# Attention by halves of the heads: logits with stationary masks in four column groups, values accumulated in transposed form

## The chip, the cores and the metric

The kernel runs on one core of one Trainium2 chip. The metric is the device time of one execution in microseconds (us). PE is TensorE, the matmul engine (PEld its weight loads), DVE is VectorE, ACT is ScalarE, POOL is GpSimd, SP the queue that starts transfers. In a matmul one operand stands still in PE (stationary, brought in by a weight load) and the columns of the other are moved past it; an eviction is the copy of a result out of the accumulator memory, PSUM. Four column groups are four matmuls of 32 stationary columns each, written 128*32 in the traces, whose results go to four separate sets of 32 rows. The granted clock (PEclk) is the share of its full clock that PE was given. Kernels are compared only within the same rounds.

## The reference, cut to what matters

Four layers in a row over x of 2048 tokens and 512 features: state-space convolution (A), attention (B), A, B. Only the attention changes.

```python
def _B_ref(x, wqkv, wo):              # x is already layer-normalised
    H = 32; Dh = 16; W, dil = 8, 2
    q, k, v = split(x @ wqkv)         # [32 heads, 2048, 16] each
    idx = pos[:, None] - (arange(W) * dil)[None, :]     # 8 keys: 0, 2, ... 14 tokens back
    logits = einsum("bhsd,bhswd->bhsw", q, k[idx]) * Dh ** -0.5    # masked to -1e9 where idx < 0
    attn = softmax(logits)            # over 8 keys
    o = einsum("bhsw,bhswd->bhsd", attn, v[idx])
    return o.reshape(B, S, D) @ wo    # the residual is added outside
```

With 8 keys per token there is no large matrix of logits. VectorE multiplies q by a shifted k elementwise; PE sums the 16 features of each head with a mask matrix ("bones"); softmax runs over 8 values; VectorE multiplies V by the probabilities, and PE sums the 8 shifts by accumulating matmuls against the identity.

## The kernel before: the parts that matter

Token t lies at partition t // 16, index j = t % 16. "ft" counts blocks of 8 heads (128 features), "fp" the two halves of the heads.

```python
def proj_qk(fp):
    for which, dst in ((0, qT[fp]), (1, kT[fp])):          # q first, then k
        for f2 in range(2):
            for sh2 in range(2):                            # whole sequence inside
                ps = psA.tile([128, 1024], F32)
                # ... 2 x 4 matmuls of 512 columns ...
                nc.scalar.copy(dst[:, f2, sh2*1024:(sh2+1)*1024], ps[:])

def qk_products(fp):
    for jh in range(2):                                     # half of the tokens
        Lp = [psL.tile([128, W, 8, 8], F32) for _ in range(2)]
        for w in range(W):
            pr = work.tile([128, 2, 1024], BF, tag="prodqk", bufs=3)
            # ... VectorE: pr = qT * (kT shifted by 2*w), one or two instructions ...
            for f2 in range(2):
                for jj in range(8):                         # product stationary, 8 columns move
                    nc.tensor.matmul(Lp[f2][:, w, jj, :], pr[:, f2, jj*128:(jj+1)*128], bones[:], ...)
        for f2 in range(2):
            nc.scalar.copy(Lsb[:, :, j0:j0+8, ft*8:(ft+1)*8], Lp[f2][:])

proj_qk(0); proj_qk(1); qk_products(0); proj_v(); qk_products(1)
# sm_pre, sm_post: softmax by halves of the tokens, all 32 heads together

def pv_group(g):                                            # 4 of the 16 token indices, all heads
    for w in range(W):
        p2 = work.tile([128, 4, D], BF, tag="prodpv", bufs=3)
        # ... VectorE: p2 = V (or its shifted copy Vp) * probabilities ...
        for jj in range(4):                                 # identity stationary, 512 columns move
            nc.tensor.matmul(po[jj//2][:, jj%2, :], ident[:], p2[:, jj, :], start=(w==0), stop=(w==7))
    # ... ScalarE: o = po

def out_group(g):
    # ... PE: 16 transposes of o, ScalarE: oT = transposes ...
    # ... PE: 5 matmuls per token index (4 of wo, 1 adds X), ScalarE: X = result

sm_pre(0); sm_pre(1); sm_post(0); pv_group(0); pv_group(1); sm_post(1)
out_group(0); pv_group(2); out_group(1); pv_group(3); out_group(2); out_group(3)
```

Instructions are emitted in this program order, but the framework that builds the kernel settles each engine's own order from this order and from what is ready.

Of the kernel before, what the change touches and what calls it, by code (L numbers as in the profile page):

```python
# [20 lines left out]
H = 32  # L21
# [51 lines left out]
def make_consts(nc, const, C):  # L73
    fc = _fft_consts()
    bones_np = np.zeros((128, 8), dtype=np.float32)
    for f in range(128):
        bones_np[f, f // 16] = 1.0
    for name in ("F1", "F1T"):
        C[name + "_h"] = nc.inline_tensor(_bf(fc[name]), name="c_" + name)
    todo = [("ident", _bf(np.eye(128)), BF), ("C2", _bf(fc["C2"]), BF), ("IC", _bf(fc["IC"]), BF),  # L80
            ("bones", _bf(bones_np), BF), ("onesr", _bf(np.ones((1, 128))), BF)]
    for i, (name, arr, dt) in enumerate(todo):
        h = nc.inline_tensor(arr, name="c_" + name)
        t = const.tile(list(arr.shape), dt, name="sb_" + name)
        nc.sync.dma_start(t[:], h.ap())
        C[name] = t
# [16 lines left out]
def store_x(nc, X, out2d):  # L103
    ov = out2d.rearrange("(p j) d -> p j d", j=NJ)
    for g in range(NG):
        (nc.sync if g % 2 == 0 else nc.scalar).dma_start(ov[:, g * 4:(g + 1) * 4, :], X[:, g * 4:(g + 1) * 4, :])


def load_b_weights(nc, tc, const, wqkv, wo):
# [14 lines left out]
    Vp = const.tile([128, NJ, D], BF, name="Vp")  # L124
    nc.vector.memset(Vp[:, 0:2, :], 0.0)
    nc.gpsimd.memset(Vp[0:1, 2:NJ, :], 0.0)
# [453 lines left out]
def b_layer(nc, tc, C, X, Wt, Vp, ln_b):  # L580
    with ExitStack() as es:
        big = es.enter_context(tc.tile_pool(name="b_big", bufs=4))
        qk = es.enter_context(tc.tile_pool(name="b_qk", bufs=1))
        small = es.enter_context(tc.tile_pool(name="b_small", bufs=2))
        work = es.enter_context(tc.tile_pool(name="b_work", bufs=2))
        sm = es.enter_context(tc.tile_pool(name="b_sm", bufs=1))
        psA = es.enter_context(tc.tile_pool(name="b_psA", bufs=2, space=PSUM))
        psT = es.enter_context(tc.tile_pool(name="b_psT", bufs=2, space=PSUM))
        psL = es.enter_context(tc.tile_pool(name="b_psL", bufs=2, space=PSUM))
# [4 lines left out]
        for g in range(NG):  # L594
            for j in range(g * 4, g * 4 + 4):
                ln_b.norm(xn[:, j, :], X[:, j, :], j)
            for hf in range(2):
                pt = psT.tile([128, 2, 4, 128], BF, name="pt_x", tag="psT")
                for jj in range(2):
                    j = g * 4 + hf * 2 + jj  # L600
                    for ct in range(4):
                        nc.tensor.transpose(pt[:, jj, ct, :], xn[:, j, ct * 128:(ct + 1) * 128], ident[:])
                s0 = (g * 4 + hf * 2) * 128
                nc.scalar.copy(xnT[:, :, s0:s0 + 256].rearrange("c t (jj p) -> c jj t p", jj=2), pt[:])  # L604
# [3 lines left out]
        def proj_qk(fp):  # L608
            for which, dst in ((0, qT[fp]), (1, kT[fp])):
                for f2 in range(2):  # L610
                    ft = fp * 2 + f2
                    for sh2 in range(2):
                        ps = psA.tile([128, 1024], F32, name="ps_qk", tag="psA")
                        for sc in range(2):
                            s0 = (sh2 * 2 + sc) * 512
                            for ct in range(4):
                                nc.tensor.matmul(ps[:, sc * 512:(sc + 1) * 512],  # L617
                                                 wqk[:, ct, which * 512 + ft * 128: which * 512 + (ft + 1) * 128],
                                                 xnT[:, ct, s0:s0 + 512], start=(ct == 0), stop=(ct == 3))
                        nc.scalar.copy(dst[:, f2, sh2 * 1024:(sh2 + 1) * 1024], ps[:])  # L620

        V = big.tile([128, NJ, D], BF, name="V", tag="big")

        def proj_v():
            for jp in range(NJ // 2):
                ps = psA.tile([128, 2, D], F32, name="ps_v", tag="psA")
                for jj in range(2):
                    j = jp * 2 + jj
                    for ct in range(4):
                        nc.tensor.matmul(ps[:, jj, :], xnT[:, ct, j * 128:(j + 1) * 128], wv[:, ct, :],  # L630
                                         start=(ct == 0), stop=(ct == 3))
                nc.scalar.copy(V[:, jp * 2:(jp + 1) * 2, :], ps[:])
            nc.sync.dma_start(Vp[1:113, 2:NJ, :], V[0:112, 2:NJ, :])
            nc.sync.dma_start(Vp[113:128, 2:NJ, :], V[112:127, 2:NJ, :])

        Lsb = sm.tile([128, W, NJ, H], BF, name="Lsb")

        def qk_products(fp):
            for jh in range(2):
                j0 = jh * 8  # L640
                Lp = [psL.tile([128, W, 8, 8], F32, name="Lp", tag="psL") for _ in range(2)]
                for w in range(W):
                    sh = DIL * w
                    pr = work.tile([128, 2, 8 * 128], BF, name="prodqk", tag="prodqk", bufs=3)
# [13 lines left out]
                    for f2 in range(2):  # L658
                        for jj in range(8):
                            nc.tensor.matmul(Lp[f2][:, w, jj, :], pr[:, f2, jj * 128:(jj + 1) * 128], bones[:],  # L660
                                             start=True, stop=True)
                for f2 in range(2):
                    ft = fp * 2 + f2
                    nc.scalar.copy(Lsb[:, :, j0:j0 + 8, ft * 8:(ft + 1) * 8], Lp[f2][:])

        proj_qk(0)
        proj_qk(1)
        qk_products(0)
        proj_v()
        qk_products(1)  # L670

        for w in range(1, W):
            nc.vector.memset(Lsb[0:1, w, 0:DIL * w, :], -1e9)
        def sm_pre(jh):
            js = slice(jh * 8, (jh + 1) * 8)
            m1 = small.tile([128, 4, 8, H], BF, name="sm_m1", tag="sm_m1")
            nc.vector.tensor_tensor(m1[:], Lsb[:, 0:4, js, :], Lsb[:, 4:8, js, :], ALU.max)
            m2 = small.tile([128, 2, 8, H], BF, name="sm_m2", tag="sm_m2")
            nc.vector.tensor_tensor(m2[:], m1[:, 0:2], m1[:, 2:4], ALU.max)
            mx = small.tile([128, 8, H], BF, name="sm_mx", tag="sm_mx")  # L680
            nc.vector.tensor_tensor(mx[:], m2[:, 0], m2[:, 1], ALU.max)
            nc.vector.tensor_tensor(Lsb[:, :, js, :], Lsb[:, :, js, :],
                                    mx[:].unsqueeze(1).to_broadcast([128, W, 8, H]), ALU.subtract)
            nc.scalar.activation(Lsb[:, :, js, :], Lsb[:, :, js, :], ACT.Exp, scale=DH ** -0.5)

        def sm_post(jh):
            js = slice(jh * 8, (jh + 1) * 8)
            s1 = small.tile([128, 4, 8, H], BF, name="sm_s1", tag="sm_m1")
            nc.vector.tensor_tensor(s1[:], Lsb[:, 0:4, js, :], Lsb[:, 4:8, js, :], ALU.add)
            s2 = small.tile([128, 2, 8, H], BF, name="sm_s2", tag="sm_m2")  # L690
            nc.vector.tensor_tensor(s2[:], s1[:, 0:2], s1[:, 2:4], ALU.add)
            den = small.tile([128, 8, H], F32, name="sm_den", tag="sm_den")
            nc.vector.tensor_tensor(den[:], s2[:, 0], s2[:, 1], ALU.add)
            rdb = small.tile([128, 8, H], BF, name="sm_rdb", tag="sm_rdb")
            with nc.allow_low_precision(reason="softmax 1/sum kept in bf16 like the reference"):
                nc.vector.reciprocal(rdb[:], den[:])
            nc.vector.tensor_tensor(Lsb[:, :, js, :], Lsb[:, :, js, :],
                                    rdb[:].unsqueeze(1).to_broadcast([128, W, 8, H]), ALU.mult)

        prob = Lsb  # L700

        o = big.tile([128, NJ, D], BF, name="o", tag="big")
        oT = big.tile([128, 4, S], BF, name="oT", tag="big")

        def pv_group(g):
            j0 = g * 4
            po = [psA.tile([128, 2, D], F32, name="po", tag="psA") for _ in range(2)]
            for w in range(W):
                sh = DIL * w
                p2 = work.tile([128, 4, D], BF, name="prodpv", tag="prodpv", bufs=3)  # L710
                ja = max(j0, sh)
                if ja < j0 + 4:
                    n = j0 + 4 - ja
                    nc.vector.tensor_tensor(  # L714
                        p2[:, ja - j0: ja - j0 + n, :].rearrange("p j (t d h) -> p (j t) d h", t=4, d=DH),
                        V[:, ja - sh: ja - sh + n, :].rearrange("p j (t d h) -> p (j t) d h", t=4, d=DH),
                        prob[:, w, ja: ja + n, :].rearrange("p j (t h) -> p (j t) h", t=4).unsqueeze(2)
# [110 lines left out]
```

## Time and profile before

The time is 694.17 us (median of 3, 694.14 to 697.09).

| second attention layer, before | us |
|---|---|
| length, first normalisation to last residual write | 147.0 |
| PE busy | 114.6 |
| VectorE busy | 94.5 |
| ScalarE busy | 64.4 |

The first attention layer lasts 147.1 us. The next lines are the busy times by stretches of the second layer: the whole layer, projections, logits with most of the softmax, and values with output. Columns: stretch in us from the start of the span, its length, then busy us (and number of instructions) of PE, PEld, DVE, ACT and POOL, then the clock granted to PE, the share of the DMA engines, GB/s.

```profile
core 0: us, PE busy (x) PEld busy (x) DVE busy (x) ACT busy (x) POOL busy (x), PEclk, DMA share, GB/s
540.70:687.70 147.00, 114.57 (x1024) 62.41 (x1040) 94.46 (x121) 64.41 (x67) 0.00 (x0) 0.88 0.08 24
540.70:576.00 35.30, 33.92 (x223) 18.34 (x228) 9.17 (x22) 23.28 (x24) 0.00 (x0) 0.94 0.00 1
576.00:626.10 50.10, 28.05 (x541) 19.58 (x545) 45.26 (x61) 17.62 (x20) 0.00 (x0) 0.73 0.14 38
626.10:687.70 61.60, 52.60 (x266) 24.49 (x271) 40.03 (x40) 23.51 (x24) 0.00 (x0) 0.97 0.07 27
```

No engine is full. In the first stretch PE works and VectorE stands; in the second VectorE works and PE is half idle. The layer is a sequence of phases. The waits of VectorE in the same layer (in total us, times, longest) name the holes:

```profile
DVE prodqk L648 <- ACT kT_7272 L620: 14.9, 1, 14.9
DVE prodqk L648 <- PE Lp L660: 12.7, 2, 11.2
DVE prodpv L714 <- PE po L728: 8.0, 2, 4.8
```

The first is the wait for the first k projection, which comes after all of q. In the second, VectorE's three product buffers are full because the logits matmuls that free them are queued behind the projections of the other half of the heads. PE's timeline of the first layer shows that queue, up to 319.6 us, where VectorE's products had stopped at 308.8 and went on at 320.0:

```profile
295.90 23.69 PE L617 MATMUL ps_qk<-xnT,wqk 128*128 128x512 bf16 x107
```

### The profile page before, as it was taken

To read this page: it belongs to the slowest core of one execution; us is meant where nothing else is said; L and a number is where in the kernel's file an instruction comes from. 1 tells how busy PE (TensorE), PEld (TensorE's weight loads), DVE (VectorE), ACT (ScalarE), POOL (GpSimd) and SP (SyncE) were. 2 spreads that over 40 slices of the span, in tenths; PEclk is the share of its full clock that TensorE was granted. 3 is DMA by queue.
4 is the path that set the end of the run, shared out by engine and by line. 5 is a ranking of instruction groups with operands and counts; after the bars stand their busy time and mean duration, and the time that the engine had idled before them with its cause. 6 is when DMAs were issued, how large, how long until landed. Compare 5 with 4: busy or idle time off the path is not lost. (4 is left out here: it accounts for less than half of the span.)

```text
span 691.4 us, 13674 instructions
## 1 busy us (share of the span) xinstructions
PE 465.4 (67%) x5930; PEld 297.7 (43%) x5977; DVE 512.5 (74%) x984; ACT 331.3 (48%) x388; POOL 8.2 (1%) x21
## 2 busy tenths in 40 slices
PE   1103656866767875599834898787796699725996
PEld 0002444544645654445521444465664446512442
DVE  6999999989989932624998985864456526989870
ACT  5980525636637454565312435555442555331335
POOL 0000000000000003000000000000000000000000
PEclk9999959979979988899955999899999899857999
DMA  9000010210210214000210000500000000300001
GB/s 307 4 0 2 32 32 2 93 33 13 82 32 19 78 63 152 1 1 1 67 43 0 1 0 4 241 1 1 1 1 0 1 1 2 106 1 1 31 31 62
DMA packets 14541, 26.69 MB, mean 39 GB/s; under 512 B 4753, under 2 KB 10258, under 8 KB 13074
## 3 DMA queue, kind: packets, MB, share of 16 engines
q1 hardware_dynamic: 11792, 23.57, 9.8%
q10 hardware_dynamic: 2688, 2.23, 1.1%
q8 instruction: 47, 0.77, 0.5%
q14 instruction: 14, 0.11, 0.1%
HBM read 13.77 MB, written 8.39 MB: 32 GB/s over the span
## 5 line engine op out<-in xcount | busy, mean ns | idle before, releaser
L728 PE MATMUL po<-prodpv,sb_ident 128*128 128x512 bf16 x248 | 65.7, 396 | 36.2 <-DVE prodpv L714 31.3
L617 PE MATMUL ps_qk<-xnT,wqk 128*128 128x512 bf16 x248 | 56.6, 379 | 1.1 <-ACT xnT L604 0.7
L193 PE MATMUL psA<-U,sb_F_128 128*128 128x128 bf16 x256 | 24.1, 242 | 47.5 <-issue 38.5
L180 ACT CAST Z<-psA 128x1024 bf16<-128x1024 f32 (+1 forms) x52 | 46.4, 960 | 20.1 <-issue 17.3
L728 PEld LDWEIGHTS <-sb_ident 128*128 128x128 bf16 x256 | 25.7, 101 | 67.5 <-issue 45.2
L180 ACT CAST xc<-psA 128x1024 bf16<-128x1024 f32 x32 | 32.0, 1012 | 44.6 <-PE psA L222 37.4
L193 PEld LDWEIGHTS <-sb_F_128 128*128 128x128 bf16 x416 | 27.1, 104 | 57.9 <-issue 50.7
L208 PE MATMUL pt<-sb_ident,Z 128*128 128x128 bf16 x384 | 38.4, 268 | 19.5 <-ACT Z L180 19.5
L714 DVE TENSOR_TENSOR prodpv<-V,Lsb 128x2048 bf16<-128x2048 bf16 (+1 forms) x40 | 42.2, 1111 | 8.2 <-PE po L728 8.0
L180 ACT CAST VT<-psA 128x512 bf16<-128x512 f32 x48 | 26.6, 588 | 44.4 <-PE psA L250 44.4
L208 PEld LDWEIGHTS <-Z 128*128 128x128 bf16 x384 | 32.8, 123 | 30.4 <-ACT Z L180 21.9
L660 PE MATMUL Lp<-sb_bones,prodqk 128*128 128x8 bf16 x1024 | 35.3, 167 | 14.7 <-DVE prodqk L656 9.4
L660 PEld LDWEIGHTS <-prodqk 128*128 128x128 bf16 x1024 | 32.9, 99 | 24.3 <-DVE prodqk L656 10.8
L247 PE MATMUL psA<-sb_IC,pa 128*128 128x256 bf16 x128 | 36.2, 283 | 9.6 <-DVE pa L262 9.6
L159 DVE TENSOR_SCALAR U<-X,ln_rstd_a,ln_nb_a 128x128 bf16<-128x128 bf16 x128 | 33.5, 307 | 7.2 <-PE psA L193 7.2
L617 PEld LDWEIGHTS <-wqk 128*128 128x128 bf16 x256 | 24.7, 98 | 29.3 <-issue 1.6
L178 DVE COPY zt<-pt 128x1024 bf16<-128x1024 bf16 x32 | 21.8, 688 | 20.6 <-PE pt L208 20.5
L248 PE MATMUL psA<-sb_IC,pb 128*128 128x256 bf16 x128 | 36.2, 283 | 1.1 <-DVE pb L263 1.1
L745 PE MATMUL ps_o<-wo_t,oT 128*128 128x512 bf16 x124 | 32.3, 379 | 6.7 <-ACT o L731 4.3
L249 PE MATMUL psA<-sb_IC,pb 128*128 128x256 bf16 x128 | 36.0, 281 | 0.0
L250 PE MATMUL psA<-sb_IC,pa 128*128 128x256 bf16 x128 | 35.9, 281 | 0.0
L467 PE MATMUL psk<-Ytab,Xtab 128*32 128x64 bf16 x1024 | 23.6, 207 | 14.4 <-issue 7.1
(175 smaller groups left out, 1100.4 us busy)
## 6 DMA issues: line engine op xcount, KB each, us to landing
Kt<-kt_scratch SPq DMA_DIRECT2D x4, 1024.0 KB, 6.9
Vp<-V SPq DMA_DIRECT2D x2, 1568.0 KB, 8.9
kt_scratch<-Kt SPq DMA_DIRECT2D x3, 1024.0 KB, 3.8
X<-in_A_u_dram SPq DMA_DIRECT2D x4, 512.0 KB, 5.5
k_scratch<-KTq SPq DMA_DIRECT2D x8, 256.0 KB, 2.0
KT<-k_scratch SPq DMA_DIRECT2D x8, 256.0 KB, 2.7
sb_F_128<-c_F SPq DMA_DIRECT2D x1, 1024.0 KB, 5.9
sb_F1T<-c_F1T SPq DMA_DIRECT2D x1, 1024.0 KB, 7.1
```

The source lines that it names most:

```text
L159: self.nc.vector.tensor_scalar(dst, src, self.rstd[:, j:j + 1], self.nb[:, j:j + 1], ALU.mult, ALU.add)
L180: self.nc.scalar.copy(dst, src)
L193: nc.tensor.matmul(o, F1[:, j, r, :], rhs_j(j), start=True, stop=not dk)
L208: nc.tensor.transpose(pt[:, r, g, :], Z[:, r, i * 4 + g, :], ident[:])
L247: nc.tensor.matmul(o, pa[:, 0, sl], IC[:, 0, :], start=True, stop=False)
L248: nc.tensor.matmul(o, pb[:, 1, sl], IC[:, 1, :], start=False, stop=False)
L249: nc.tensor.matmul(o, pb[:, 0, sl], IC[:, 2, :], start=False, stop=False)
L250: nc.tensor.matmul(o, pa[:, 1, sl], IC[:, 2, :], start=False, stop=True)
L617: nc.tensor.matmul(ps[:, sc * 512:(sc + 1) * 512], wqk[:, ct, which * 512 + ft * 128: which * 512 + (ft + 1) * 128], xnT[:, ct, s0:s0 + 51 ...
L660: nc.tensor.matmul(Lp[f2][:, w, jj, :], pr[:, f2, jj * 128:(jj + 1) * 128], bones[:], start=True, stop=True)
L714: nc.vector.tensor_tensor(p2[:, ja - j0: ja - j0 + n, :].rearrange("p j (t d h) -> p (j t) d h", t=4, d=DH), V[:, ja - sh: ja - sh + n, :] ...
L728: nc.tensor.matmul(po[jj // 2][:, jj % 2, :], ident[:], p2[:, jj, :], start=(w == 0), stop=(w == W - 1))
```

## The change

Its intent: make logits cheaper on PE, get rid of the transposes of o, and let the two halves of the heads overlap, so that one engine's phase covers the other's. The core of the diff, with cuts marked:

```diff
-    bones_np = np.zeros((128, 8), dtype=np.float32)
+    bones_np = np.zeros((128, 4, 32), dtype=np.float32)
     for f in range(128):
-        bones_np[f, f // 16] = 1.0
+        for k in range(4):
+            bones_np[f, k, 8 * k + f // 16] = 1.0
 # ... small and work pools: 4 product buffers shared by logits and values; PSUM split anew ...
 # ... xnT: every second eviction goes to VectorE instead of ScalarE ...
-            for which, dst in ((0, qT[fp]), (1, kT[fp])):
-                for f2 in range(2):
-                    for sh2 in range(2):                 # 1024-column evictions
+            for sh2 in range(2):
+                for which, dst in ((1, kT[fp]), (0, qT[fp])):
+                    for f2 in range(2):                  # 512-column evictions
 # ... in qk_products:
-                    for f2 in range(2):
-                        for jj in range(8):
-                            nc.tensor.matmul(Lp[f2][:, w, jj, :], pr[:, f2, jj * 128:(jj + 1) * 128], bones[:],
-                                             start=True, stop=True)
+                    for hb in range(2):
+                        for f2 in range(2):
+                            r0 = (hb * 2 + f2) * 32
+                            nc.tensor.matmul(Lp[r0:r0 + 32, w // 4, :], bones[:, w % 4, :],
+                                             pr[:, f2, hb * 512:(hb + 1) * 512], start=(w % 4 == 0),
+                                             stop=(w % 4 == 3), skip_group_check=True)
+                LT = small.tile([128, 2, 4, 128], BF, name="LT", tag="LT", bufs=2)
+                nc.scalar.copy(LT[:]..., Lp[:]...)
+                # 8 PE transposes of LT into pt, then
+                nc.scalar.copy(L[fp][:, :, j0:j0 + 8]..., pt[:]...)
 # ... softmax(fp): by halves of the heads; the edge memsets go to GpSimd ...
 # ... pv(fp, jh): half of the heads and half of the tokens per block:
-                for jj in range(4):
-                    nc.tensor.matmul(po[jj // 2][:, jj % 2, :], ident[:], p2[:, jj, :],
-                                     start=(w == 0), stop=(w == W - 1))
+                for f2 in range(2):
+                    for jj in range(8):
+                        nc.tensor.matmul(po[f2][:, jj, :], p2[:, jj, f2 * 128:(f2 + 1) * 128], ident[:],
+                                         start=(w == 0 and jj % 4 == 0), stop=(w == W - 1), skip_group_check=True)
+            for f2 in range(2):
+                nc.scalar.copy(oT[:, fp * 2 + f2, j0 * 128:(j0 + 8) * 128], po[f2][:]...)
 # ... out(jh): no transposes; stores each 4 token indices as soon as they are done ...
         proj_qk(0)
+        qk_products(0)
         proj_qk(1)
-        qk_products(0)
+        softmax(0)
         proj_v()
         qk_products(1)
+        softmax(1)
+        pv(0, 0)
+        pv(0, 1)
+        pv(1, 0)
+        out(0)
+        pv(1, 1)
+        out(1)
```

So there are three parts: a new form of the logits on PE (the mask stationary, 512 product columns moving, four 32-row outputs in four column groups), a new form of the values (the product stationary, the result already transposed), and a new structure (halves of the heads throughout, and a new order).

## The prediction

> **What bounds the kernel now.** The change touches only the two attention layers. By the timeline each lasts 147 us from first normalisation to last residual write (284.9 to 432.0, 540.7 to 687.7); the rest stays. By stretches of time, in the second layer VectorE is busy 94.5 of 147 us, PE 114.6, ScalarE 64.4: nothing is full, the layer is a sequence of phases. In the first 35.3 us (projections) PE is busy 33.9, VectorE 9.2; in the next 50.1 us (logits, softmax) VectorE 45.3, PE 28.1 at a granted clock of 0.73; in the last 61.6 us (values, output) PE 52.6, VectorE 40.0. The waits show VectorE's holes per layer: 14.9 us for the first K projection, 12.7 us because the logits matmuls were queued behind the projections, 8.0 us on the value matmuls; PE waits 15.7 us through the softmax.
>
> **What the change does, per layer.**
> - Order: projections go by sequence halves, K first; logits of the first head half come before the second half's projections. VectorE's first product should start about 13 us into the layer instead of 20, without the 12.7 us hole; the first softmax runs under remaining projections.
> - Logits on PE: 512 weight loads with 8-column matmuls (16 take 0.5 us: 15 us) become 128 matmuls of 512 columns in four column groups, plus 32 transposes (55 ns each). The Trainium skill, "TensorE: Matmul & The Clock Gate", Part 3, says such column tiles run concurrently (2.38x for three). This trace agrees: the filter-table matmuls in four groups issue four per 30 ns, although 64 columns alone need about 27. Estimate: 0.25 us for four, plus mode changes: 8 to 12 us.
> - Values on PE: 128 matmuls at 0.215 us (27.5 us) become 512 of 128 columns at 55 ns (28 us): equal. The 64 transposes of o (3.5 us) and 8 of their evictions (1.01 us each) go.
> - ScalarE: smaller evictions (0.59 us for 512 columns, 1.01 for 1024) cost 5 us, logits 3; 8 us of oT and 4 us of xnT copies go. About 62 us, not binding.
> - VectorE: same products (2048 elements, 1.15 us each), a few more splits, 2.7 us of xnT copies, memsets moved away: about 96 us. The probabilities are read in runs of 8 with stride 32; I expect the same rate.
>
> **Sum.** VectorE 96 us, about 8 us hole at the start, 4 us of stalls, and a tail of about 16 us with PE alone (the second value half shares PE with out(0), then out(1), 8 x 1.08 us): 124 us per layer. PE, about 108 us, fits with little slack. Gain 23 us per layer, 46 in all; the store's tail (3.7 us) stays. Nearly all of the gain is waiting removed, not work.
>
> **Predicted: 648 us, 8 in 10 between 630 and 668.** Faster by over 2%: 0.93; within 2%: 0.04; slower: 0.03.
>
> **What would show it.** Layers of about 124 us; VectorE's first logit product about 13 us in; its wait for logits matmuls nearly gone; four 512-column logits matmuls within 0.3 us; value products still 1.2 us; 16 value matmuls about 0.9 us; the last 10 us PE alone.
>
> **What would make it wrong.** Column groups that serialise (0.85 us for four: +12 us PE per layer). V projections late, so that the 9 us copy to Vp delays the values. Value accumulators held until two 1 us copies end, at four blocks, stalling PE about 2.5 us each. PE at half clock entering the value phase (16 matmuls 1.7 us against 1.15). A slow strided read of the probabilities would double 37 us per layer.

## The result, and the profile after

The changed kernel takes 664.15 us (median of 4, 661.57 to 664.47) beside 695.63 us of the kernel before in the same rounds. The ratio is 0.9539 (95% interval 0.9501 to 0.9577). Ratios here are the mean time of one kernel's fast runs over that of the other's fast runs of the same rounds, so not quite the ratio of the medians quoted. The outputs are correct.

The second attention layer now lasts 131.4 us (526.67 to 658.08), the first 131.1. That is 15.6 and 16.0 us less, together 31.6, which is the whole gain. (The spans of the two profiled runs differ by only 29.2 us, because the part between the layers, which the change leaves alone, is 1.9 us longer in the changed kernel's profile.) The stretches of the second layer: the whole, up to the first value product, from there to the end, and the last 10.7 us.

```profile
526.67:658.08 131.41, 114.91 (x999) 66.87 (x1008) 96.11 (x130) 61.29 (x87) 2.22 (x14) 0.93 0.08 27
526.67:594.40 67.73, 61.25 (x398) 27.28 (x405) 52.06 (x76) 40.48 (x60) 1.57 (x11) 0.95 0.09 25
594.40:658.08 63.68, 53.66 (x601) 39.59 (x603) 44.05 (x56) 20.80 (x27) 0.65 (x3) 0.91 0.08 29
647.40:658.08 10.68, 9.67 (x50) 4.04 (x48) 0.00 (x0) 6.50 (x10) 0.00 (x0) 1.00 0.12 49
```

Three things are to be seen. The work did not shrink: PE is busy 114.9 us in the layer (114.6 before), VectorE 96.1 (94.5). All of the gain lies before VectorE's first value product: 67.7 us instead of 85.4 (540.7 to 626.1); from there on the layer takes 63.7 us instead of 61.6. And in that first part PE is now busy 61.3 of 67.7 us, nearly full. VectorE's waits in the second layer:

```profile
DVE prod L642 <- ACT qT_7308 L615: 6.6, 1, 6.6
DVE prod_8499 L713 <- PE po L728: 6.4, 1, 6.4
DVE prod L642 <- PE Lp L655: 3.6, 1, 3.6
DVE prod L650 <- PE Lp L655: 2.5, 2, 1.3
DVE prod L650 <- ACT kT_7311 L615: 2.2, 1, 2.2
DVE sm_m_7895 L681 <- POOL L_7314 L670: 1.7, 1, 1.7
```

With VectorE the layer can be added up. Its length is VectorE's busy time, its waits and what remains after its last product: 94.5 + 38.8 + 13.4 us before, 96.1 + 23.7 + 11.5 us after (0.3 and 0.1 us are short gaps). So 15.1 of the 15.6 us are waiting removed.

The hole at the start fell from 14.9 to 6.6 us, and the wait for logits matmuls from 12.7 to 6.1 (3.6 and 2.5), less than the prediction hoped. The timeline of PE in the first layer shows why that wait stays: V projections stand ahead of the second half's logits.

```profile
331.29 1.05 PE L655 MATMUL Lp<-prod,sb_bones 128*32 128x512 bf16 x16
334.47 10.53 PE L623 MATMUL ps_v<-wv,xnT 128*128 128x512 bf16 x47
344.93 1.04 PE L655 MATMUL Lp<-prod,sb_bones 128*32 128x512 bf16 x15
```

During the 10.5 us of V projections no logits matmul runs. VectorE is busy 7.3 us of it, 3.7 with three more products and the rest with the softmax of the first half, then stands; its own timeline says what it waited for:

```profile
345.37 4.36 DVE L642 TENSOR_TENSOR prod<-qT_4691,kT_4693 128x2048 bf16<-128x2048 bf16 x4 [3.60 <-PE Lp L655]
```

The first of these groups also settles a point of the prediction: 16 logits matmuls of 512 columns took 1.05 us together, while 16 of 512 columns at 0.215 us each would be 3.4 us. The four column groups do run at the same time. (The 27 ns that the prediction gives for 64 columns are 0.215 us x 64/512, an estimate.) The value matmuls are as priced, a set of 16 every 0.89 us in PE's timeline of the first layer:

```profile
399.58 1.06 PE L728 MATMUL po<-sb_ident,prod_5825 128*128 128x128 bf16 x16
400.48 1.06 PE L728 MATMUL po<-sb_ident,prod_5843 128*128 128x128 bf16 x16
401.37 1.06 PE L728 MATMUL po<-sb_ident,prod_5861 128*128 128x128 bf16 x16
```

### The profile page after: what moved, and what is told of

Its sections match the earlier page's. It is cut to its first block, busy times and chain, and to the rows that moved or that the text cites. A ratio compares the mean times of both kernels' runs of the same rounds, so it can differ in the third digit from the quotient of the medians.

```text
span 662.2 us, 13624 instructions
## 1 busy us (share of the span) xinstructions
PE 467.0 (71%) x5880; PEld 306.2 (46%) x5913; DVE 516.4 (78%) x1001; ACT 325.2 (49%) x428; POOL 12.6 (2%) x49
## 3 DMA queue, kind: packets, MB, share of 16 engines
q1 hardware_dynamic: 12334, 24.65, 10.5%
## 5 line engine op out<-in xcount | busy, mean ns | idle before, releaser
L613 PE MATMUL ps_qk<-xnT,wqk 128*128 128x512 bf16 x246 | 61.2, 380 | 1.6 <-ACT kT_4692 L615 0.3
L731 ACT CAST oT<-po 128x1024 bf16<-128x1024 f32 x16 | 15.4, 1015 | 58.7 <-PE po L728 58.7
L613 PEld LDWEIGHTS <-wqk 128*128 128x128 bf16 x256 | 22.8, 98 | 29.5 <-issue 8.2
L464 PE MATMUL psk<-Y2tab,Xtab 128*32 128x48 bf16 x1024 | 22.6, 203 | 13.3 <-issue 11.4
L655 PE MATMUL Lp<-prod,sb_bones 128*32 128x512 bf16 x256 | 24.7, 392 | 10.3 <-DVE prod L650 7.5
L213 PE MATMUL psA<-zt,sb_C_120 128*128 128x512 bf16 x48 | 22.7, 473 | 11.2 <-DVE zt L172 6.0
L140 DVE BATCH_NORM_STATS2 ln_st_b<-X 128x6 f32<-128x384 bf16 (+1 forms) x64 | 21.3, 413 | 11.4 <-ACT X L272 11.4
```

What stands on the lines that cost most here:

```text
L140: self.nc.vector.bn_stats(self.st[:, j, part, :], X[:, j, a:b])
L613: nc.tensor.matmul(ps[:], wqk[:, ct, f0:f0 + 128], xnT[:, ct, s0:s0 + 512], start=(ct == 0), stop=(ct == 3))
L655: nc.tensor.matmul(Lp[r0:r0 + 32, w // 4, :], bones[:, w % 4, :], pr[:, f2, hb * 512:(hb + 1) * 512], start=(w % 4 == 0), stop=(w % 4 == 3 ...
```

## The experiments

Two theories were set against each other. Theory O: the gain is the order, which fills VectorE's holes; the new forms hardly matter. Rival F: the gain is the cheaper forms on PE and ScalarE. Beside each time stands the length of the second attention layer in its profile, because the parts that the variants leave alone differ by some microseconds from one profile to the next: in the profiles of all these runs the first attention layer starts 282.7 to 287.4 us into the span, and between the two attention layers lie 107.9 to 110.6 us.

| run | us, median | ratio to before (95%) | second layer, us |
|---|---|---|---|
| kernel before | 693.9 to 697.3 | 1 | 147.0 |
| changed kernel | 664.15 | 0.9539 (0.9501 to 0.9577) | 131.4 |
| changed kernel again | 664.54 | 0.9542 (0.9498 to 0.9585) | 131.4 |
| old logits form | 657.50 | 0.9460 (0.9428 to 0.9491) | 128.6 |
| old values form | 666.15 | 0.9600 (0.9568 to 0.9632) | 133.0 |
| both old forms | 660.77 | 0.9488 (0.9455 to 0.9522) | 130.1 |
| old order | 681.48 | 0.9819 (0.9797 to 0.9841) | 141.0 |
| kernel before, new order | 695.75 | 1.0023 (1.0002 to 1.0044) | 147.0 |
| 8 product buffers | 656.89 | 0.9443 (0.9401 to 0.9485) | 127.9 |
| value blocks in another order | 659.11 | 0.9467 (0.9432 to 0.9502) | 130.2 |
| first softmax emitted late | 660.70 | 0.9493 (0.9450 to 0.9537) | 130.8 |
| combined | 651.37 | 0.9354 (0.9321 to 0.9388) | 125.5 |
| combined, V early | 667.04 | 0.9577 (0.9545 to 0.9610) | 133.8 |
| combined, V early, values first | 670.88 | 0.9630 (0.9585 to 0.9676) | 135.4 |

### 1. The old logits form in the changed kernel

```diff
-                    for hb in range(2):
-                        for f2 in range(2):
-                            nc.tensor.matmul(Lp[r0:r0 + 32, w // 4, :], bones[:, w % 4, :], ...)
-                # ... LT copy, 8 transposes, L copy ...
+                    for f2 in range(2):
+                        for jj in range(8):
+                            nc.tensor.matmul(Lp[:, f2, w, jj, :], pr[:, f2, jj * 128:(jj + 1) * 128],
+                                             bones[:, 0, 0:8], start=True, stop=True)
+                for f2 in range(2):
+                    for q in range(2):
+                        nc.scalar.copy(L[fp][:, q, j0:j0 + 8, f2, :, :]..., Lp[:, f2, q * 4:(q + 1) * 4])
```

> The changed kernel with the logits as before: products stationary, 8 moving columns, no transposes; order and all else kept. Theory O (the gain is the order, which fills VectorE's holes): the PE cost of logits goes from about 8 to about 15 us per layer but most of it hides under VectorE; 664 to 672 us. Rival F (the gain is the cheaper forms on PE and ScalarE): at least 10 of the 31 us lost, 674 us or more.

Measured: 657.50 us, ratio 0.9460. Its interval lies below those of both runs of the changed kernel, so undoing this part makes the kernel faster, by 2.4 us in the first layer and 2.8 us in the second. Neither theory had expected that. Two things in the traces explain it. The first is PE's cadence while logits alternate with projections. In the changed kernel (timeline of PE, first layer):

```profile
316.23 0.40 PE L655 MATMUL Lp<-prod,sb_bones 128*32 128x512 bf16 x4
316.56 1.04 PE L613 MATMUL ps_qk<-xnT,wqk 128*128 128x512 bf16 x4
317.53 0.40 PE L655 MATMUL Lp<-prod,sb_bones 128*32 128x512 bf16 x4
318.83 0.40 PE L655 MATMUL Lp<-prod,sb_bones 128*32 128x512 bf16 x4
```

and with the old form:

```profile
308.26 0.54 PE L654 MATMUL Lp<-sb_bones,prod 128*128 128x8 bf16 x16
308.66 1.02 PE L613 MATMUL ps_qk<-xnT,wqk 128*128 128x512 bf16 x4
309.52 0.55 PE L654 MATMUL Lp<-sb_bones,prod 128*128 128x8 bf16 x16
310.79 0.54 PE L654 MATMUL Lp<-sb_bones,prod 128*128 128x8 bf16 x16
```

One shift of logits and four projection matmuls come every 1.30 us in the new form (316.23, 317.53, 318.83) and every 1.26 to 1.27 us in the old. The new form streams its four matmuls at once, but the four projection matmuls need 0.86 us of the 1.30, which leaves 0.44 us for the logits; four column groups alone need about 0.22 by the group of 16 above (its sets of four start 0.21 to 0.23 us apart). The other 0.22 us come where the array changes between column groups and the whole: the first logits matmul starts 0.309 us after the last projection matmul, and the next projection matmul 0.323 us after the last logits matmul, where two matmuls of one kind lie 0.216 us apart. In the old form, which has no column groups, those two steps take 0.215 and 0.025 us. The Trainium skill, "TensorEngine Tiling (Array Packing)", Key Properties, says that changing the tiling mode drains the engine; this trace fits that, with about 0.1 us each way. It does not tell such a drain from a weight load that is no longer hidden: elsewhere here a weight load starts with the matmul before it, but at these two points only right at the change (317.526 and 317.856), and takes 0.09 to 0.10 us. So where logits alternate with projections, the new form saves nothing on PE.

The second is the way from the last logits matmul to the softmax. In the changed kernel, first layer, second half of the heads (timeline of all engines):

```profile
352.99 1.01 ACT L659 CAST LT<-Lp 128x1024 bf16<-128x1024 f32 x1 [4.36 <-PE Lp L655]
354.19 1.06 PE L663 MATMUL pt_l<-sb_ident,LT 128*128 128x128 bf16 x8
355.29 1.01 ACT L664 COPY L_4696<-pt_l 128x1024 bf16<-128x1024 bf16 x1 [1.28 <-PE pt_l L663]
356.35 0.65 POOL L670 MEMSET L_4696<- 1x160 bf16 x3 [7.21 <-ACT L_4696 L664]
357.04 0.69 DVE L681 TENSOR_TENSOR sm_m_5277<-L_4696 128x1024 bf16<-128x1024 bf16 x1 [1.61 <-POOL L_4696 L670]
```

and with the old form:

```profile
352.29 1.20 ACT L658 CAST L<-Lp 128x256 bf16<-128x256 f32 x4 [6.20 <-PE Lp L654]
353.55 0.65 POOL L664 MEMSET L<- 1x160 bf16 x3 [7.20 <-ACT L L658]
354.23 0.69 DVE L675 TENSOR_TENSOR sm_m<-L 128x1024 bf16<-128x1024 bf16 x1
```

From the start of the eviction to the first softmax instruction it is 4.05 us in the new form (352.99 to 357.04) and 1.94 us in the old (352.29 to 354.23): a second trip through PE and ScalarE, at a point where VectorE has little else to do.

VectorE's waits say where the 2.8 us lie. In the second layer VectorE is busy 96.1 us with either form and needs 11.5 us from its last product to the end, but it waits 23.7 us with the new form and 20.9 with the old. These are its waits with the old form that differ from the list above (the 2.2 us on k are gone):

```profile
DVE prod L642 <- PE Lp L654: 3.9, 1, 3.9
DVE sm_m L675 <- POOL L L664: 1.8, 1, 1.8
DVE prod L650 <- PE Lp L654: 1.3, 1, 1.3
```

The 1.8 us on sm_m are at the first softmax. At the second, VectorE waits 1.7 us in the new form, and none there and 0.3 us a little later in the old: 1.4 us of the 2.8 are the longer way. The other 1.4 were lost earlier: VectorE goes on after the V projections 60.6 us into the layer instead of 59.2, and PE begins them at 43.0 us instead of 42.0, having had no gap above 0.3 us since the tenth microsecond of the layer in either form. How these 1.4 us divide between the changes of mode, the transposes and the evictions was not shown by undoing each alone.

### 2. The old values form in the changed kernel

```diff
-                for f2 in range(2):
-                    for jj in range(8):
-                        nc.tensor.matmul(po[f2][:, jj, :], p2[:, jj, f2 * 128:(f2 + 1) * 128], ident[:], ...)
+                for jq in range(4):
+                    nc.tensor.matmul(po[jq // 2][:, (jq % 2) * 2:(jq % 2) * 2 + 2, :], ident[:],
+                                     p2[:, jq * 2:jq * 2 + 2, :], start=(w == 0), stop=(w == W - 1))
+            # ... copy to o, 16 transposes, copy to oT ...
```

> The changed kernel with the values as before (identity stationary, 512 moving columns, then transposes of o and a second eviction), order and halves of the heads kept. Theory O: PE +3.5 us and ScalarE +8 us per layer, partly in the tail where PE is alone: 666 to 674 us. Rival F: half or more of the gain lost, 680 us or more.

Measured: 666.15 us, ratio 0.9600, second layer 133.0 us against 131.4. The interval just touches that of the changed kernel. The transposed form is worth 2.2 us in the first layer and 1.6 in the second, inside what theory O said, and far from half the gain.

### 3. The old order with both new forms

```diff
         proj_qk(0)
-        qk_products(0)
         proj_qk(1)
-        softmax(0)
+        qk_products(0)
         proj_v()
         qk_products(1)
+        softmax(0)
         softmax(1)
 # and in proj_qk: q before k, whole sequence inside, as before
```

> The changed kernel with both new forms, but projections emitted as before (all projections of q and k before the first logits, q before k, whole sequence inside). Theory O: the first logit product moves from 14 us into the layer to 20 or later and the wait of VectorE for logits matmuls returns; 684 us or more. Rival F: 672 us or less.

Measured: 681.48 us, ratio 0.9819, clearly slower than the changed kernel and clearly faster than the kernel before. It falls between the two expectations. VectorE's waits of the second layer show the two old holes again, 11.8 us at the first projection and 11.7 us on logits matmuls:

```profile
DVE prod L642 <- ACT kT L615: 11.8, 1, 11.8
DVE prod L650 <- PE Lp L655: 11.7, 3, 10.4
```

So the order is needed for more than half of the gain. But even in the old order the rest of the change, both new forms included, is worth 6 us per layer (141.0 against 147.0).

### 4. The kernel before with only the new order

```diff
-            for which, dst in ((0, qT[fp]), (1, kT[fp])):
-                for f2 in range(2):
-                    for sh2 in range(2):
+            for sh2 in range(2):
+                for which, dst in ((1, kT[fp]), (0, qT[fp])):
+                    for f2 in range(2):
 ...
         proj_qk(0)
-        proj_qk(1)
         qk_products(0)
+        proj_qk(1)
         proj_v()
```

> The kernel before with only the order of projections and first logits taken from the change (by halves of the sequence, k first; first logits before the second half of the projections). Both old forms kept, softmax as before. Theory O: VectorE's 14.9 and 12.7 us holes shrink to 7 to 8 and 1 to 4 us, so 10 to 16 us per layer less, 664 to 676 us. Rival F: 690 us or more.

Measured: 695.75 us, ratio 1.0023: nothing. Theory O falls in its plain form: the order alone gives no gain. The hole did not go, it moved. VectorE waits 38.8 us in the second layer, as before. Its wait at the start did shrink (14.9 to 9.7 us), but then PE runs all 64 V projection matmuls in a row before the second half's logits; first PE's timeline of the second layer, then VectorE's:

```profile
584.77 13.98 PE L630 MATMUL ps_v<-wv,xnT 128*128 128x512 bf16 x64
```

```profile
599.17 0.43 DVE L648 TENSOR_TENSOR prodqk<-qT,kT 128x512 bf16<-128x512 bf16 x1 [15.29 <-PE Lp L660]
```

With its three product buffers full, VectorE stands for 15.3 us. In the kernel before, softmax runs over all heads at once, so it cannot begin until the second half's logits are there, and VectorE has nothing else. In the changed kernel the softmax of the first half is ready at that point and runs during the V projections.

### 5. Both old forms in the new structure

The edits of experiments 1 and 2 together.

> The changed kernel with both old forms (logits with 8 moving columns; values with stationary identity and transposes of o), but its order and its halves of the heads. From the two single runs (old logits 5 us faster, old values 4 us slower than the changed kernel) 658 to 664 us, so the whole gain would be structure and order. If a form is worth more than the single runs show, 668 us or more.

Measured: 660.77 us, ratio 0.9488, second layer 130.1 us against 131.4, first layer 131.7 against 131.1. With both old forms the changed kernel keeps its whole gain. Rival F falls: in this structure the forms together are worth nothing. (In the old structure they were not tried alone.) What remains is the structure. This run and experiment 4 have the same forms and nearly the same order of projections and logits, and lie 35 us apart. Between them stand the halves of the heads in softmax and values, and also four shared product buffers instead of three, smaller evictions, half of the xnT copies on VectorE and the early stores. Those smaller items were not taken apart. The buffers are the nearest rival, since the 15.3 us stand of experiment 4 is a wait with all buffers full: one buffer more holds one product more, 1.14 us of VectorE's work from start to start, so by this estimate the fourth buffer alone can put off little of that stand; but no run tried it.

### 6. The first softmax emitted late

```diff
         proj_qk(1)
-        softmax(0)
         proj_v()
         qk_products(1)
+        softmax(0)
         softmax(1)
```

> The changed kernel with the first half's softmax emitted only after the second half's logits (just before the second softmax). Theory S (the new order pays only because the softmax of the first half of the heads is there to fill VectorE while PE runs the V projections): VectorE's wait for logits matmuls there grows from 3.6 us by about 6 us per layer, 672 to 680 us. Rival (the softmax's place does not matter, since VectorE's total is what ends the layer): within 3 us of the changed kernel.

Measured: 660.70 us, ratio 0.9493, second layer 130.8 us: not slower. But this run does not test theory S. In the trace the first softmax has hardly moved, since it was ready and the engine's order is filled with what is ready. In the first layer it begins 43.1 us into the layer instead of 40.5, and its instructions still lie between the products of the second half and during the V projections. Its first instruction, in the changed kernel and here:

```profile
325.48 0.69 DVE L681 TENSOR_TENSOR sm_m_5025<-L_4695 128x1024 bf16<-128x1024 bf16 x1
```

```profile
328.61 0.68 DVE L681 TENSOR_TENSOR sm_m<-L 128x1024 bf16<-128x1024 bf16 x1
```

What was moved in the program moved little on the engine. That the first softmax is what pays for the new order is therefore argued from experiments 4 and 5 and from the traces, and not shown by an experiment that takes it away alone.

### 7. The changed kernel again, and more product buffers

> The changed kernel itself once more, so that the variants of this call are compared on one chip: ratio 0.954 again, 662 to 665 us. If the faster old logits of the run before were only the chip, this one comes out near 657 here.

Measured: 664.54 us, ratio 0.9542; the repeat agrees.

```diff
-        work = es.enter_context(tc.tile_pool(name="b_work", bufs=4))
+        work = es.enter_context(tc.tile_pool(name="b_work", bufs=8))
```

> The changed kernel with 8 buffers of products instead of 4. Theory B (VectorE stands still for 3.6, 1.3 and 1.2 us per layer because its four buffers are full while PE runs V projections): these waits go and about 3 us per layer are won, 656 to 660 us. Rival P (PE's own work ends the layer, buffers only move VectorE's waiting): the waits go too, but the time stays within 2 us of the changed kernel.

Measured: 656.89 us, ratio 0.9443, second layer 127.9 us. Theory B holds: the waits of VectorE for logits matmuls (6.1 us) are gone from its list, and 3.5 us per layer are won. The waits that are left, second layer:

```profile
DVE prod L642 <- ACT qT L615: 8.0, 2, 6.6
DVE sm_m L681 <- POOL L L670: 2.9, 2, 1.9
DVE sm_s L691 <- ACT L L689: 2.1, 1, 2.1
```

The 2.2 us wait on k is gone too. Not all of these 8.3 us come back as time, because other waits grow: 1.4 us on q, 1.2 us on the edge memsets, 2.1 us on the exponentials. The 6.4 us wait on value matmuls has also gone, but it lay in the tail, where VectorE had time to spare: what remains of the layer after VectorE's last product grew by as much, from 11.5 to 18.0 us.

### 8. Another order of the value blocks

```diff
         pv(0, 0)
-        pv(0, 1)
         pv(1, 0)
+        pv(0, 1)
         out(0)
         pv(1, 1)
         out(1)
```

> The changed kernel with the value blocks in the order (half 0, tokens 0), (half 1, tokens 0), then (half 0, tokens 1), out(0), (half 1, tokens 1), out(1), so that out(0) can fill PE while VectorE sets the pace. Theory: the 6.4 us wait of VectorE on value matmuls in the tail shrinks and PE's idle before it (about 0.24 us per product) is used; 2 to 3 us per layer, 658 to 660 us. Rival (PE's total in the tail is the same, so nothing): within 1 us of the changed kernel.

Measured: 659.11 us, ratio 0.9467. The time is inside the expectation, but the profile does not carry it: the second layer is 130.2 us, 1.2 us less than the changed kernel's, and the wait on value matmuls only went from 6.4 to 5.4 us. The intervals of the two kernels also overlap a little. A gain of about 1 us per layer is what the trace supports; the rest of the difference lies in parts that this edit does not touch.

### 9. Combined, and V earlier

The old logits form, 8 buffers and the new order of value blocks together:

> Old logits form, 8 product buffers and the new order of value blocks together in the changed kernel. If the three savings are apart (6, 5 and 5 us), 647 to 651 us; if they share one wait, 653 us or more.

Measured: 651.37 us (650.77 to 652.68), ratio 0.9354, second layer 125.5 us. It is correct and beats both kernels. The savings do not quite add up: 2.8, 3.5 and 1.2 us per layer would be 7.5, and 5.9 came. PE's longest wait in its second layer is before the value blocks:

```profile
PE po L722 <- DVE prod L707: 10.5, 2, 9.9
```

So two variants put the V projections before the second half's q and k:

```diff
         proj_qk(0)
         qk_products(0)
+        proj_v()
         softmax(0)
         proj_qk(1)
-        proj_v()
         qk_products(1)
         softmax(1)
```

> The combined version with the V projections emitted before the second half's q and k projections. Its trace had PE idle for 9.9 us before the value blocks, after V projections that ended late and a copy of V that takes 9 us. Theory: with V early the value blocks start earlier and the layer gets 3 to 5 us shorter, 641 to 646 us. Rival: the second logits get later by as much, within 2 us of 651.

> As the run before, with the first value block emitted ahead of the second softmax and both output blocks last. If PE's idle before the value blocks is what is left, 638 to 645 us; if VectorE is full there, no better than the run before.

Measured: 667.04 us (0.9577) and 670.88 us (0.9630), both slower than the combined version. For the first, 667 lies outside both expectations; the rival named the right cause, later second logits, but put its cost far too low. VectorE has made the last product of the first half 34 us into the first layer, while PE still runs V projections, and gets the second half's q only at 53 us. Its waits in the first layer of the first variant:

```profile
DVE prod L642 <- ACT qT L615: 10.9, 2, 6.6
DVE sm_m L675 <- POOL L L664: 4.5, 2, 4.3
DVE sm_s L685 <- ACT L L683: 3.6, 1, 3.6
```

The second wait for q is 4.3 us, and the first softmax waits 4.3 and 3.6 us at steps that other work covered before. PE's wait before the values did go (10.5 us in the combined version, 3.7 here, second layer), but it was not the limit: filling it cost VectorE more.

## Why the prediction was right or wrong

The time, 664 us, lies in the range of 630 to 668, 4 us from its slow end. The direction and the mechanism (waiting removed) held, but the gain is 31 us where 46 was said.

- "Nearly all of the gain is waiting removed, not work": right. PE is busy 114.9 us in the layer against 114.6, VectorE 96.1 against 94.5. The forecast 96 us for VectorE and 62 for ScalarE were measured as 96.1 and 61.3. PE was forecast at about 108 and is busy 114.9: the saving on PE that the new forms were to bring is not seen there.
- First product of VectorE about 13 us into the layer: 14.4 (285.02 to 299.37 in the first layer). Close.
- Value products 1.2 us and 16 value matmuls 0.9 us: right, 1.22 to 1.23 and 0.89. The strided read of the probabilities costs nothing that the trace shows. The Trainium skill, "VectorE: DVE Perf Modes", The perf-mode tier table, gives 1224 ns for a bf16 tensor_tensor of 2048 elements, and this trace agrees with 1.22.
- Four logits matmuls in four column groups within 0.3 us: right about running together (16 in 1.05 us), but beside projections the visit costs 0.44 us with its two mode changes. The prediction expected the new form to cut PE's logits from 15 to 8 to 12 us per layer and counted its 32 transposes as 1.8 us of PE work. PE is busy 17.6 us with the old form in the kernel before, and 12.6 with the new one plus 2.9 with its transposes. The prediction did not count the longer way from logits to softmax. In this kernel the form is a loss of 2.4 to 2.8 us per layer.
- The step that failed is the sum: "about 8 us hole at the start, 4 us of stalls, and a tail of about 16 us". VectorE's idle time in the second layer, 131.4 minus 96.1, is 35.3 us. It divides into 6.6 us at the start, 10.4 us of stalls (3.6, 2.5, 2.2, 1.7 and 0.4 us), a tail of about 18 us (6.4 us waiting on value matmuls with full buffers, and 11.5 us after its last product), and 0.4 us of short gaps. The term that was mis-sized is the stalls: 10 us instead of 4. The tail is 2 us longer, and the start 1.4 us shorter. That makes 131 instead of 124.
- "its wait for logits matmuls nearly gone": wrong, 6.1 us stayed. The sum in the prediction saw that PE "fits with little slack" but did not draw the conclusion: with PE busy 61.3 of the first 67.7 us, each run of projections on PE stops VectorE as soon as its four buffers are full. Eight buffers removed these waits and gave 3.5 us per layer.
- "V projections late, so that the 9 us copy to Vp delays the values": the risk was named and came true in another form: PE's V projections held up VectorE's products of the second half by 3.6 us. The copy to Vp is not among the waits shown above.
- "PE at half clock entering the value phase": came true in small. In the first layer two sets of 16 value matmuls took 1.80 and 1.91 us at a granted clock of 0.55 (360.0 to 363.5), against 1.06 later.
- "The last 10 us PE alone": right. In the last 10.7 us VectorE does nothing and PE is busy 9.7.

What the prediction never asked is which of the three parts carries the gain. The order alone carries none (695.75 us), the forms together none (660.77 us without them), the new forms and the rest of the structure in the old order 6 us per layer (681.48 us), and the new order together with that rest all of it. That the halves of the heads are what counts in that rest is the reading of the traces; its smaller items were not taken apart.

## What to carry to other kernels

When two engines take turns, changing the order moves a hole unless the idle engine has other work that is ready; here the halves of the heads seem to make that work, as argued above. Judge a new operation form by undoing it alone in the finished kernel: here a form that runs four matmuls at once lost to the old one, because of what surrounds it (a second trip before the next step, and on PE changes of mode that ate what it saved). And before trusting a test of order, check in the trace that the order on the engine changed.

## What the Trainium skill lacked or had wrong

- "TensorEngine Tiling (Array Packing)", Key Properties, says that a change of tiling mode drains the engine but gives no cost. Here a visit of four column groups between whole-array matmuls cost 0.44 us, of which about 0.22 us lie at the two changes (0.309 and 0.323 us from start to start, where two matmuls of one kind lie 0.216 us apart). The trace does not show whether that is the drain or the weight loads, which start only there.
- "TensorE: Matmul & The Clock Gate", Part 3, has a measured speedup of 2.38 for three column tiles and none for four. Here 16 matmuls of 512 columns over four column groups took 1.05 us, against 3.4 us at 0.215 us each: 3.3 times, the end of the last ones counted in. From start to start a set of four came every 0.21 to 0.23 us, about 4 times.
- The same page, Back-to-back issue gap, gives about 81 ns per matmul with its weight load at 128 columns and about 131 ns at 512 as sustained rates. Here 16 matmuls of 128 columns, each with its own weight load, come every 0.89 us (56 ns each), and 64 of 512 columns, each with its own weight load, took 13.98 us (218 ns each). Both fit what the page calls the isolated gap.
